# Retention in 64-token steps on 64x64 array tiles, with casting loads of q, k and weights on the Pool queue

## The chip, the core and the metric

The kernel runs on one core of a Trainium2 chip. The metric is the device time of one execution in microseconds (us): the median of three runs is 377.36 us (377.29 to 378.0).

## The reference

A retention layer (attention with an exponential decay in place of softmax) feeds a bilinear feed-forward block, written FFN below. q, k and v are float32 of shape [8, 8, 576, 64] (batch, head, sequence, head width); the weights are [512, 1536], [512, 1536] and [1536, 512].

```python
scores = scale * np.matmul(q, k.transpose(0, 1, 3, 2))
gamma = 1.0 - 2.0 ** (-5.0 - np.arange(H))
Dmat = np.where(rel >= 0, gamma[:, None, None] ** rel, 0.0)     # rel = i - j
attn = np.matmul(scores * Dmat, v)
x = attn.transpose(0, 2, 1, 3).reshape(B * S, H * D)            # [4608, 512]
out = ((x @ w_a) * (x @ w_b)) @ w_out
```

## The kernel before

The 4608 tokens are 36 chunks of 128. Two batches are nine chunks (PER = 9); the middle one (MID) holds the last 64 tokens of one batch and the first 64 of the next. The decay splits: v is scaled by gamma^-j (`vs`), the retention output by scale times gamma^i (`qs`), so that the products between need only a causal mask.

Retention of a chunk, heads in four pairs (HP):

- `load` (L97): q, k and v as float32 on SP's queue, three DMAs of 256 KB, each of 1024 runs of 256 B; five buffers of each.
- `cast` (L182): q and k to bf16 (for the first chunks on ACT and DVE, L187 and L188; later on POOL, L190 and L191), v times `vs` on POOL (L192).
- `transposes` (L199): eight 128x128 transposes on PE, then copies to `qkT`.
- `state` (L216): per head pair one product k^T v of 128 rows by 128 columns, summed over the chunks of a batch in one PSUM tile, whose two diagonal blocks ACT copies out (L232, L233).
- `scores` (L235): eight products, a head in each 64-row half of the array, masked by DVE (L250).
- `outputs` (L258): eight products of v with the masked scores (L267) and eight of the state with q (L276), each of 64 columns of the array; DVE multiplies by `qs` into `xT` (L282).

The FFN (`ffn_block`, L290) takes blocks of 512, 256, 384, 384 and then 512 tokens. Per block and each of 12 columns of 128 there are four matmuls into pa (L300) and four into pb (L313), ACT copies pa (L306), DVE multiplies (L318); then 12 matmuls per 128 tokens with w_out (L326), a copy to `osb` (ACT or DVE, L335 and L337) and a store on SP's queue (L338). One FFN matmul of 512 tokens is called a unit below: a block of 512 tokens has 144 of them, the kernel 1296.

What sets the order: the schedule is manual, so instructions stand on each engine as the code emits them. Chunks 0 to 3 come first, one after the other. The weights are loaded by casting DMAs on POOL's queue (`load_w`, `load_wo`). A small DMA (`gate`, L366) on SP's queue reads loaded w_out, so that SP's loads of chunks 4 and up wait for it. Later stages are placed among the FFN matmuls by `todo`, a list of places counted in units: chunks 4 to 8 one at a time (`one_by_one`), the others in pairs (`first_stage`: transposes and state; `second_stage`: state and scores; `third_stage`: outputs).

Of the kernel before, what the change touches and what calls it, by code (L numbers as in the profile page):

```python
# [18 lines left out]
def kernel(  # L19
# [18 lines left out]

    nc = tc.nc

    B, H, S, D = q.shape
    DM = H * D
# [9 lines left out]
    PER = 2 * S // 128  # L52
    MID = PER // 2
    HALF = S - 128 * MID
    assert HALF == 64 and NTOK % (2 * S) == 0

    def rows_of(i):

        b, m = 2 * (i // PER), i % PER
        if m < MID:  # L60
            return [(0, 128, b, 128 * m)]
        if m == MID:
            return [(0, 64, b, 128 * m), (64, 64, b + 1, 0)]
        return [(0, 128, b + 1, 64 + 128 * (m - MID - 1))]

# [6 lines left out]
    stage = pool("stage", 5)  # L72
    nat = pool("nat", 5)
    qkt_pool = pool("qkt", 4)
    st_pool = pool("st", 4)
    h_pool = pool("hT", 2)
    ha_pool = pool("ha", 6)
    o_pool = pool("osb", 4)
    PS = bass.MemoryType.PSUM
    ps_ffn = pool("ps_ffn", 3, PS)  # L80
    ps_att = pool("ps_att", 4, PS)
    ps_kv = pool("ps_kv", 1, PS)
# [3 lines left out]
    wa_r = moe_w_a.rearrange("(c p) f -> p c f", p=128)  # L86
    wb_r = moe_w_b.rearrange("(c p) f -> p c f", p=128)
    wo_r = moe_w_out.rearrange("(c p) m -> p c m", p=128)
# [3 lines left out]
    xT = big.tile([128, HP, NTOK], BF16)  # L92


    staged = {}

    def load(i):  # L97
        if i >= NCH:
            return
        tiles = []  # L100
        for name, src in (("qf", q), ("kf", k), ("vf", v)):
            t = stage.tile([128, DM], FP32, tag=name, name=name)
            for r0, n, b, s0 in rows_of(i):
                nc.sync.dma_start(  # L104
                    t[r0:r0 + n, :].rearrange("p (h d) -> p h d", h=H),
                    src[b, :, s0:s0 + n, :].rearrange("h s d -> s h d"))
            tiles.append(t)
        staged[i] = tiles

    for i in range(4):  # L110
        load(i)


    idxp_i = const.tile([128, PER], INT32)
    nc.gpsimd.iota(idxp_i[:, 0:MID + 1], pattern=[[128, MID + 1]], base=0,
# [3 lines left out]
    idx_i = const.tile([128, S + 64], INT32)  # L119
    nc.gpsimd.iota(idx_i[:, 0:S], pattern=[[1, S]], base=0,  # L120
                   channel_multiplier=0)
    nc.gpsimd.iota(idx_i[:, S:S + 64], pattern=[[1, 64]], base=0,
                   channel_multiplier=0)
    identity = const.tile([128, 128], BF16)
    make_identity(nc, identity)
    mask = const.tile([128, 128], BF16)
    nc.gpsimd.memset(mask, 1.0)
    nc.gpsimd.affine_select(
        out=mask, in_=mask, compare_op=ALU.is_ge, fill=0.0,
        base=0, pattern=[[1, 128]], channel_multiplier=-1)  # L130
    mask2 = const.tile([128, 128], BF16)
    nc.gpsimd.tensor_copy(mask2, mask)
    nc.gpsimd.memset(mask2[0:64, 64:128], 0.0)

    lgp = const.tile([128, HP], FP32)
    for c in range(HP):
        nc.vector.memset(lgp[0:64, c:c + 1], math.log(gammas[2 * c]))
        nc.vector.memset(lgp[64:128, c:c + 1], math.log(gammas[2 * c + 1]))
    biasq = const.tile([128, 1], FP32)
    nc.vector.memset(biasq, math.log(scale))  # L140
    idxp_f = const.tile([128, PER], FP32)
# [7 lines left out]
    idx_f = const.tile([128, S + 64], FP32)  # L149
    nc.vector.tensor_copy(idx_f, idx_i)  # L150
    qs = const.tile([128, HP, S + 64], FP32)

    def make_qs(c):
        nc.scalar.activation(qs[:, c, :], idx_f, AF.Exp,
                             bias=biasq[:, 0:1], scale=lgp[:, c:c + 1])

    states = [const.tile([128, HP, 128], BF16, name=f"state{i}")
              for i in range(4)]
    for t in states:
        nc.vector.memset(t, 0.0)  # L160
# [55 lines left out]
    def state(i):  # L216
        m = i % PER
        if m == PER - 1:
            return
# [259 lines left out]
```

## Time and profile before

| what | value |
|---|---|
| median of 3 runs | 377.36 us (377.29 to 378.0) |
| profiled execution: span from first to last instruction | 375.4 us; the median run is 2.0 us longer |
| PE busy | 345.6 us (92%) |
| DVE, ACT, POOL busy | 172.5, 127.9, 77.8 us |
| DMA: HBM read, written | 37.75 MB, 9.44 MB |
| retention products on PE | 1248 (288 transposes among them) |

The page has the busy share of each engine, its course over 40 slices of the span, the DMA queues, the chain of work that ended last, and groups of instructions by line. L300 is line 300 of the kernel; PE is the matmul engine, PEld its weight loads, SPq and POOLq are DMA issues. A matmul's printed duration covers its way through the pipeline; what it costs on a busy PE is the distance between two starts. A few matmul records are missing.

### The profile page before, as it was taken

The page shows a single profiled execution, that of the slowest core. Times are in us where ns is not written, and L with a number is a line of the kernel's source. Part 1 is how long each engine was busy: PE and PEld are TensorE (multiplying, and loading weights), DVE is VectorE, ACT ScalarE, POOL GpSimd, SP SyncE. Part 2 cuts the span into 40 slices and gives each one's busy share as a digit, 9 for nine tenths or more (in the row PEclk, how much of TensorE's full clock was granted, in tenths as well). Part 3 has the DMA queues.
Part 4 walks back from the last instruction along what each step waited for, and adds up shares of the span by engine and source line. Part 5 has one row for each costly group of instructions (what it writes and reads, how often), then busy time and mean ns, then how long its engine had stood idle before and what let it go on. Part 6 is the DMA issues. An engine that isn't in the chain of part 4 may idle for free.

```text
span 375.4 us, 6629 instructions
## 1 busy us (share of the span) xinstructions
PE 345.6 (92%) x2604; PEld 186.4 (50%) x2640; DVE 172.5 (46%) x292; ACT 127.9 (34%) x248; POOL 77.8 (21%) x113
## 2 busy tenths in 40 slices
PE   2669987777999999999999999999999999999995
PEld 1444443555565565455455545454545454544442
DVE  4542344454555546246434553455445544532421
ACT  7323313432452443244215422442244234303320
POOL 3550032542142230314031403040403000000000
PEclk9999999899999999999999999999999999999999
DMA  9999899957970890395039403950510020011002
GB/s 174 188 206 207 166 204 257 225 116 142 230 164 0 190 228 5 106 223 95 28 119 222 83 30 109 193 120 30 144 27 3 36 77 0 2 56 58 1 28 84
DMA packets 122511, 42.90 MB, mean 114 GB/s; under 512 B 113264, under 2 KB 117872, under 8 KB 122480
## 3 DMA queue, kind: packets, MB, share of 16 engines
q1 hardware_dynamic: 117728, 37.76, 47.5%
q0 software_dynamic: 4752, 4.72, 7.8%
q8 instruction: 20, 0.33, 0.4%
q14 instruction: 11, 0.09, 0.1%
HBM read 37.75 MB, written 9.44 MB: 126 GB/s over the span
## 4 chain that ended last, share of the span: by engine, by line
PE 78%; DMA 7%; SPq 6%; DVE 3%; issue 2%; POOL 1%; ACT 1%; DVEq 0%
PE po L326 23%; PE pa L300 22%; PE pb L313 21%; SPq L104 6%; DMA wo_sb<-in_moe_w_out_dram 5%; PE tp L204 4%; PE o L267 3%; DMA vf<-in_v_dram 3%; PE kv L227 2%; PE o L276 2%; DVE sT L250 1%; DVE hT L318 1%; ACT qkT L208 1%; DVE qkT L209 0%; POOL wa_sb L163 0%
## 5 line engine op out<-in xcount | busy, mean ns | idle before, releaser
L318 DVE TENSOR_TENSOR hT<-ha,pb 128x512 bf16<-128x512 bf16 (+2 forms) x120 | 76.1, 634 | 112.9 <-PE pb L313 106.8
L300 PE MATMUL pa<-xT,wa_sb 128*128 128x512 bf16 (+2 forms) x467 | 112.4, 364 | 2.9 <-DVE xT L282 1.6
L313 PE MATMUL pb<-xT,wb_sb 128*128 128x512 bf16 (+2 forms) x475 | 111.3, 359 | 0.2
L306 ACT CAST ha<-pa 128x512 bf16<-128x512 f32 (+2 forms) x120 | 65.1, 543 | 126.1 <-PE pa L300 112.6
L326 PE MATMUL po<-wo_sb,hT 128*128 128x512 bf16 x414 | 94.5, 379 | 2.0 <-issue 1.6
L192 POOL TENSOR_TENSOR vb<-vf,vs 128x512 bf16<-128x512 f32 x36 | 37.5, 1043 | 177.9 <-PE o L267 61.1
L313 PEld LDWEIGHTS <-wb_sb 128*128 128x128 bf16 x480 | 47.2, 98 | 46.8 <-issue 0.2
L300 PEld LDWEIGHTS <-wa_sb 128*128 128x128 bf16 x480 | 45.4, 99 | 45.8 <-issue 4.5
L326 PEld LDWEIGHTS <-hT 128*128 128x128 bf16 x432 | 40.8, 98 | 47.4
L337 DVE COPY osb<-po 128x512 f32<-128x512 f32 x17 | 11.8, 692 | 53.2 <-PE po L326 53.2
L335 ACT COPY osb<-po 128x512 f32<-128x512 f32 x19 | 11.1, 585 | 69.2 <-PE po L326 68.1
L282 DVE TENSOR_TENSOR xT<-o,qs 128x512 bf16<-128x512 f32 x36 | 24.3, 685 | 9.3 <-PE o L276 8.1
L267 PE MATMUL o<-sT,vb 128*64 128x128 bf16 x288 | 16.7, 231 | 7.6 <-DVE sT L250 7.4
L190 POOL CAST qb<-qf 128x512 bf16<-128x512 f32 x27 | 16.7, 618 | 23.1 <-issue 18.4
L204 PE MATMUL tp<-identity,qb 128*128 128x128 bf16 x144 | 15.0, 231 | 6.2 <-ACT qb L187 6.2
L267 PEld LDWEIGHTS <-vb 128*64 128x64 bf16 x288 | 11.0, 114 | 16.5 <-issue 13.1
L191 POOL CAST kb<-kf 128x512 bf16<-128x512 f32 x27 | 16.6, 613 | 8.7 <-DVE hT L318 4.0
L211 ACT COPY qkT<-tp 128x1024 bf16<-128x1024 bf16 x14 | 14.2, 1012 | 11.4 <-PE tp L204 11.4
L204 PE MATMUL tp<-identity,kb 128*128 128x128 bf16 x144 | 15.1, 232 | 1.5 <-DVE kb L188 1.5
L204 PEld LDWEIGHTS <-qb 128*128 128x128 bf16 x144 | 10.5, 102 | 11.1 <-ACT qb L187 7.4
L244 PEld LDWEIGHTS <-qkT 64*128 64x128 bf16 x288 | 8.8, 98 | 10.5 <-DVE qkT L209 8.2
L227 PE MATMUL kv<-vb,kb 128*128 128x128 bf16 (+1 forms) x128 | 13.3, 230 | 0.0
(197 smaller groups left out, 191.1 us busy)
## 6 DMA issues: line engine op xcount, KB each, us to landing
out_dram<-osb SPq DMA_DIRECT2D x36, 256.0 KB, 2.0
qf<-in_q_dram SPq DMA_DIRECT2D x32, 256.0 KB, 4.9
kf<-in_k_dram SPq DMA_DIRECT2D x32, 256.0 KB, 5.1
vf<-in_v_dram SPq DMA_DIRECT2D x32, 256.0 KB, 5.1
wo_sb<-in_moe_w_out_dram POOLq DMA_DIRECT2D x3, 512.0 KB, 17.4
qf<-in_q_dram SPq DMA_DIRECT2D x8, 128.0 KB, 4.1
kf<-in_k_dram SPq DMA_DIRECT2D x8, 128.0 KB, 3.6
vf<-in_v_dram SPq DMA_DIRECT2D x8, 128.0 KB, 4.1
```

The source lines that it names most:

```text
L104: nc.sync.dma_start(t[r0:r0 + n, :].rearrange("p (h d) -> p h d", h=H), src[b, :, s0:s0 + n, :].rearrange("h s d -> s h d"))
L190: nc.gpsimd.tensor_copy(qb, qf)
L192: nc.gpsimd.tensor_tensor(vb.rearrange("p (h d) -> p h d", h=H), vf.rearrange("p (h d) -> p h d", h=H), vs[:, i % PER, :].unsqueeze(2).to_ ...
L204: nc.tensor.transpose(tp[:, w, p, :], src[:, p * 128:(p + 1) * 128], identity)
L227: nc.tensor.matmul(kv[:, p, :], kb[r, sl], vb[r, sl], start=(m in (0, MID) and p == 0), stop=True, skip_group_check=True)
L267: nc.tensor.matmul(o[64 * hi:64 * hi + 64, p, :], vb[:, e0:e0 + 64], sT[:, hi, p, :], start=(p == 0), stop=(m == 0), skip_group_check=True)
L282: later.append(lambda: nc.vector.tensor_tensor(xT[:, :, i * 128:(i + 1) * 128], o, qs[:, :, s0:s0 + 128], op=ALU.mult))
L300: nc.tensor.matmul(pa[:, 0:n], wa_sb[:, c, fs], xT[:, c, tok0:tok0 + n], start=(c == 0), stop=(c == NC - 1))
L306: nc.scalar.copy(ha[:, 0:n], pa[:, 0:n])
L313: nc.tensor.matmul(pb[:, 0:n], wb_sb[:, c, fs], xT[:, c, tok0:tok0 + n], start=(c == 0), stop=(c == NC - 1))
L318: nc.vector.tensor_tensor(hT[:, F, 0:n], has[F][:, 0:n], pb[:, 0:n], op=ALU.mult)
L326: nc.tensor.matmul(po, hT[:, F, u * 128:(u + 1) * 128], wo_sb[:, F, :], start=(F == 0), stop=(F == NF - 1))
```

## The change

Retention is rewritten; the FFN's matmuls stay as they are.

- The step is 64 tokens. A chunk of 128 still is loaded at once and holds two steps, s = 0 and 1. Each product is 64 by 64 by 64 and uses one quarter of the array; four in a row use the four quarters. Per chunk there are 16 products k^T v, 16 scores (only within a step), 16 of v with scores, and 16 of the state with q: 2240 in the kernel. The state is no longer summed in PSUM: DVE adds each step's k^T v to a float32 sum (L268, L270), and ACT or POOL casts it to bf16 (`sbf`, L275, L277).
- q and k are loaded by casting DMAs on POOL's queue (L102) into a bf16 tile; the casts on ACT, DVE and POOL go. v stays on SP's queue.
- From chunk 6 on the transposes are DMAs on SP's queue (L231). The first six chunks keep the transposes on PE (L238).
- The chunk order is new: chunks 0 to 3 first, 4 and 5 singly in the first FFN block, then pairs (units[6] is chunks 6 and 7). `todo` has two places for a pair: `first` (stage1: state with q, scores; then the DMA transposes of the next pair, the scaling of v and the loads for later pairs) and `second` (stage2: the rest of the outputs; then k^T v of the next pair).
- The weight loads are cut into columns 0-255, 256-639, 640-1023, 1024-1535, each of four DMAs of 64 partitions; small DMAs (`hold`) on SP's queue make its loads of v wait for those of q. Heads stand in another order in `xT`, and the rows of w_a and w_b follow it.
- The FFN blocks are all 512 tokens, with block 1 cut in pieces (128, 128, 256, 256). PSUM: four tiles for the FFN instead of three. Eleven matmuls on zeros (`idle_products`) are added among the first chunks. The last store is split over two queues.

The diff, cut to its core:

```diff
+    def load_qk(i):
+        t = nat.tile([128, 2, DM], BF16, tag="qk", name="qk")
+        for w, src in ((0, q), (1, k)):
+            for r0, n, b, s0 in rows_of(i):
+                nc.gpsimd.dma_start(
+                    t[r0:r0 + n, w, :].rearrange("p (h d) -> p h d", h=H),
+                    src[b, :, s0:s0 + n, :].rearrange("h s d -> s h d"))
...
+    def transposes(i, by_dma):
...
+        if by_dma:
+            nc.sync.dma_start_transpose(
+                qkT.rearrange("p w c t -> p (w c) t"),
+                qk.rearrange("p w e -> p (w e)"))
+            return
...
+    def kv(unit, conv):
...
+                    for r in (0, 1):
+                        e = slice(64 * (2 * p + r), 64 * (2 * p + r) + 64)
+                        nc.tensor.matmul(ps[s][half(r), ci, p, :],
+                                         kb[half(s), e], vb[half(s), e],
+                                         start=True, stop=True,
+                                         skip_group_check=True)
...
+                nc.vector.tensor_tensor(new, ps[s][:, ci], last_sum[0],
+                                        op=ALU.add)
...
+    def from_state(o, ci, i, h, s, start):
+        r, p, c, j = h % 2, h // 2, h // 4, h % 4
+        u = 2 * i + s
+        st = state_of[u] if u % STEPS else zero_state
+        nc.tensor.matmul(o[s][half(c), ci, j, :], st[half(r), p, :],
+                         qkt_of[i][half(r), 0, p, half(s)],
+                         start=start, stop=True, skip_group_check=True)
...
+    def stage1(unit):
...
+                        nc.tensor.matmul(sc[r][half(s), ci, p, :],
+                                         qkT[half(r), 1, p, half(s)],
+                                         qkT[half(r), 0, p, half(s)],
...
+    def stage2(unit):
...
+                        nc.tensor.matmul(
+                            o[s][half(c), ci, j, :],
+                            vb[half(s), 64 * h:64 * h + 64],
+                            sT[half(s), h % 2, ci, h // 2, :],
...
+    idle_products(7)
+    for i in range(4):
+        vscale(i, nc.vector)
+        transposes(i, False)
+        kv((i,), nc.scalar)
+        flush()
+        if i == 0:
+            make_qs(0, EARLY)
+            load_w(0, 256)
+            load_w(256, 640)
+        if i:
+            stage2((i - 1,))
+        stage1((i,))
+        if i == 3:
+            idle_products(4)
+    stage2((3,))
+    hold(3, wa_sb[0:1, 0, 640 - 64:640])
...
+    def ahead(g):
+        if g + 1 < len(units) and g + 1 >= 6:
+            for i in units[g + 1]:
+                transposes(i, True)
...
+    def first(g):
+        flush()
+        stage1(units[g])
+        ahead(g)
+
+    def second(g):
+        flush()
+        stage2(units[g])
+        if 6 <= g + 1 < len(units):
+            kv(units[g + 1], nc.gpsimd)
...
+    todo = [(52, begin_single, (4,)), (58, first, (4,)), (68, second, (4,)),
+            (56, make_qs, (EARLY, QCOLS)),
+            (80, begin_single, (5,)), (86, first, (5,)), (94, second, (5,)),
+            (130, first, (6,)), (150, second, (6,))]
+    for g in range(7, len(units)):
+        p = 288 + 144 * ((units[g][0] - 8) // 4)
+        if units[g][0] % 4 == 0:
+            todo += [(p - 86, first, (g,)), (p - 66, second, (g,))]
...
+            todo += [(p - 40, first, (g,)), (p - 20, second, (g,))]
```

Two places show how the change moves instructions. The first is POOL's queue around the weight loads. Before, it holds the scaling of v (vb) and all weights, and no load of q or k (128x4x384 is the shape of a DMA; x3 means three alike in a row):

```order
L132 COPY mask_135<-mask 128x128
L133 MEMSET mask_135 64x64
L192 TENSOR_TENSOR vb<-vf,vs 128x512 x3
L163 DMA wa_sb<-in_moe_w_a_dram 128x4x384
L164 DMA wb_sb<-in_moe_w_b_dram 128x4x384
L192 TENSOR_TENSOR vb<-vf,vs 128x512
L163 DMA wa_sb<-in_moe_w_a_dram 128x4x512
L164 DMA wb_sb<-in_moe_w_b_dram 128x4x512
L163 DMA wa_sb<-in_moe_w_a_dram 128x4x640
L164 DMA wb_sb<-in_moe_w_b_dram 128x4x640
L167 DMA wo_sb<-in_moe_w_out_dram 128x4x512 x3
```

Now it holds the loads of q and k of chunks 0 to 3, then the weights up to column 1023, and then the following, of which the first two rows are chunk 4 (in two halves), the fifth and sixth chunk 5, the last two chunk 6:

```order
L102 DMA qk<-in_q_dram 64x8x64 x2
L102 DMA qk<-in_k_dram 64x8x64 x2
L118 DMA wa_sb<-in_moe_w_a_dram 64x4x512 x2
L118 DMA wb_sb<-in_moe_w_b_dram 64x4x512 x2
L102 DMA qk<-in_q_dram 128x8x64
L102 DMA qk<-in_k_dram 128x8x64
L124 DMA wo_sb<-in_moe_w_out_dram 128x4x512 x3
L439 IOTA idx_i 128x64
L441 IOTA idx_i 128x576
L443 IOTA idx_i 128x128
L102 DMA qk<-in_q_dram 128x8x64
L102 DMA qk<-in_k_dram 128x8x64
```

So chunks 4 and 5 have moved ahead of the last weights, and chunks 6 and 7 stand behind all of them in the same queue.

The second place is SP's queue behind the gate. Before, chunk 4 (in halves), then chunk 5, with q, k and v in turn:

```order
L104 DMA vf<-in_v_dram 128x8x64
L366 DMA gate<-wo_sb 1x16x4
L104 DMA qf<-in_q_dram 64x8x64 x2
L104 DMA kf<-in_k_dram 64x8x64 x2
L104 DMA vf<-in_v_dram 64x8x64 x2
L104 DMA qf<-in_q_dram 128x8x64
L104 DMA kf<-in_k_dram 128x8x64
```

Now v alone, and between the loads of v the transposes of chunks 6 and 7, then of 8 and 9, and so on:

```order
L138 DMA gate<-wa_sb 1x16x4
L110 DMA vf<-in_v_dram 64x8x64 x2
L110 DMA vf<-in_v_dram 128x8x64 x7
L231 DMA_TRANSPOSE qkT<-qk 128x8x128 x2
L110 DMA vf<-in_v_dram 128x8x64
L110 DMA vf<-in_v_dram 64x8x64 x2
L231 DMA_TRANSPOSE qkT<-qk 128x8x128 x2
L110 DMA vf<-in_v_dram 128x8x64 x2
L409 DMA out_dram<-osb 128x512 x4
```

The gate waits for columns up to 639 of w_a instead of for w_out; seven loads of v stand ahead of the first transposes, and the stores of a block's output queue behind transposes and loads of v.

544 lines of the change are left out of this document (264 added, 280 removed).

## The prediction

> **What bounds the kernel now.** I read the page first, for the busy shares and their course.
>
> ```profile
> span 375.4 us, 6629 instructions
> PE 345.6 (92%) x2604; PEld 186.4 (50%) x2640; DVE 172.5 (46%) x292; ACT 127.9 (34%) x248; POOL 77.8 (21%) x113
> PE   2669987777999999999999999999999999999995
> DMA  9999899957970890395039403950510020011002
> q0 software_dynamic: 4752, 4.72, 7.8%
> PE 78%; DMA 7%; SPq 6%; DVE 3%; issue 2%; POOL 1%; ACT 1%; DVEq 0%
> ```
>
> From the eleventh slice on (94 us) PE is full; before that DMA is, and PE has holes. So there are two stages with two limits. The table by windows (us; PE busy; ... ; granted clock, DMA share, GB/s) puts numbers to them, and the chain in order of time gives starts on PE.
>
> ```profile
> 4.00:16.00 12.00, 7.20 (x71) 5.09 (x72) 6.24 (x11) 6.76 (x12) 4.20 (x5) 1.00 1.34 218
> 20.00:40.00 20.00, 17.23 (x98) 8.57 (x96) 6.67 (x11) 5.53 (x11) 3.59 (x5) 1.00 1.23 206
> 26.42:95.00 68.58, 58.81 (x441) 32.76 (x446) 27.62 (x52) 21.78 (x45) 17.54 (x22) 0.98 0.96 189
> ```
>
> ```profile
> 12.34 4.93 DMA vf<-in_v_dram
> 22.06 17.37 DMA wo_sb<-in_moe_w_out_dram
> 156.28 0.86 PE pa L300 x4
> 158.88 0.86 PE pb L313 x4
> 181.73 6.85 PE po L326 x31
> 293.35 6.85 PE po L326 x31
> ```
>
> *The full stage.* From 156.28 to 158.88 twelve matmuls start: 0.217 us each; with the rounding of the starts I take 0.216 for a unit. The same place of the block comes three blocks later at 293.35: (293.35 - 181.73) / 3 = 37.21 us a block. Its 144 units are 31.10; the other 6.11 us are two pairs of chunks, 3.06 us a pair. All 1296 units are 279.9 us, which the change leaves.
>
> *The start.* The first FFN matmul comes at 26.42 us, and until 95 us PE is idle for 68.58 - 58.81 = 9.8 us. This is the timeline of PE, whose first two rows are the same product in two chunks:
>
> ```profile
> 17.54 0.29 PE L244 MATMUL sc_298<-qkT 64*128 64x128 bf16 x1 [1.14 <-DVE qkT L209]
> 22.64 0.29 PE L244 MATMUL sc_355<-qkT 64*128 64x128 bf16 x1 [1.14 <-DVE qkT L209]
> 26.42 0.58 PE L300 MATMUL pa<-xT,wa_sb 128*128 128x512 bf16 x1 [0.78 <-DVE xT L282]
> 27.23 4.12 PE L300 MATMUL pa<-xT,wa_sb 128*128 128x512 bf16 x10 [0.22 <-issue]
> 75.04 0.24 PE L267 MATMUL o<-sT,vb 128*64 128x128 bf16 x1 [0.46 <-DVE sT L250]
> 75.97 0.25 PE L267 MATMUL o<-sT,vb 128*64 128x128 bf16 x2 [0.69 <-DVE sT L250]
> ```
>
> A chunk takes 5.10 us, while the twelve loads of the first four chunks have landed at 12.34 + 4.93 = 17.27. Ten matmuls then take 4.12 us, about half speed. The two last rows are the waits of a chunk that is done alone among FFN matmuls: 1.15 us.
>
> **The full stage after the change.** These are PE rows of one pair:
>
> ```profile
> 196.45 0.39 PE L204 MATMUL tp<-identity,qb 128*128 128x128 bf16 x4
> 197.56 1.03 PE L300 MATMUL pa<-xT,wa_sb 128*128 128x512 bf16 x3
> 211.10 0.39 PE L267 MATMUL o<-sT,vb 128*64 128x128 bf16 x8
> 211.32 0.29 PE L276 MATMUL o<-qkT,state_165 128*64 128x64 bf16 x8
> 218.17 0.23 PE L244 MATMUL sc_2835<-qkT 64*128 64x128 bf16 x1
> 218.17 0.23 PE L244 MATMUL sc_2836<-qkT 64*128 64x128 bf16 x1
> 218.23 0.22 PE L244 MATMUL sc_2835<-qkT 64*128 64x128 bf16 x1
> ```
>
> and from the rows of line 276, one product 64 wide (min/median/max ns):
>
> ```profile
> L276 PE MATMUL o<-qkT,state_165 x8: 192/196/196, 211.3 to 211.4; 128*64 128x64 bf16 x8
> ```
>
> Before: 16 transposes and 4 whole products take 197.56 - 196.45 = 1.11 us, 0.0555 each. Products on half the array go two at a time: in two row halves both start at 218.17 and the next at 218.23; in two column halves eight start in 211.32 - 211.10 = 0.22 us, 0.028 each. A pair is 20 x 0.0555 + 4 x 0.0555 + 16 x 0.028 + 32 x 0.028 = 2.68 us. The rest of the 3.06, 0.38 us, I put to the passages between whole-array and part-array products, two visits a pair; the new kernel has two visits as well (`first`, `second`).
>
> After: 128 products, 32 groups of four. The eight 64-wide products of 211.32 print 0.29 us in all and 0.196 for one: seven distances in 0.094 us, 0.0135 each, 0.027 a couple. Four quarters at once are not in this trace. If they run together, a group costs as a couple does; the floor I set at 0.031, for 0.02 of rounding in 0.29. If only couples run together, 0.062. Both kinds of couple overlap in these rows, so I take 0.036, near the floor. A pair is 32 x 0.036 + 0.38 = 1.53 us (1.37 to 2.36), and fifteen pairs 23.0 us (20.6 to 35.5).
>
> The transposes' cover: they are issued in `first` of the pair before. For eight pairs (units 6, and every second one from 10) about 46 units lie between, 46 x 0.216 = 9.9 us and the products between, 11 us; for the others 98 units. A DMA transpose is not in this trace. Nearest is a load of 256 KB, on SP's queue:
>
> ```profile
> DMA to landing us min/median/max: 3.3/5.1/5.2
> ```
>
> It lands 3.3 us after issue alone and at most 5.2 behind others; in a row one comes every 1.2 us (256 KB at the 218 GB/s of the 4 to 16 us window). Two transposes at that price take 5 to 6.4 us, at four times the pieces 4 x 2.4 + 4 = 13.6. I take twice, 4.8 + 4 = 8.8 us, under 11; the upper end costs 2.6 x 8 = 21 us. The Trainium skill (DMA: Bandwidth & Descriptors, "Latency and other measured facts") gives 261 GB/s for DMA transposes; that would be an estimated 1.0 us for 256 KB and leave the sum as it is, and no run here shows it.
>
> DVE gains two adds a chunk and two halved multiplies each for masks and output. Rows by form:
>
> ```profile
> L318 DVE TENSOR_TENSOR hT<-ha,pb 128x512 bf16<-128x512 bf16 x84 | 57.8, 688 | 88.1 <-PE pb L313 86.7 <-PE pa L300 1.3
> L282 DVE TENSOR_TENSOR xT<-o,qs 128x512 bf16<-128x512 f32 x36 | 24.3, 685 | 9.3 <-PE o L276 8.1 <-PE o L267 1.2
> L318 DVE TENSOR_TENSOR hT<-ha,pb 128x256 bf16<-128x256 bf16 x12 | 5.0, 417 | 9.1 <-PE pb L313 6.7 <-ACT ha L306 2.4
> L209 DVE COPY qkT<-tp 128x512 bf16<-128x512 bf16 x9 | 3.8, 425 | 11.9 <-ACT qkT L208 11.9
> L154 ACT ACTIVATE qs<-idx_f,biasq,lgp 128x640 f32<-128x640 f32 x4 | 3.6, 912 | 0.0
> L163 POOL DMA_DIRECT2D wa_sb<-in_moe_w_a_dram x3 | 2.5, 838 | 0.0
> L337 DVE COPY osb<-po x2: 691/692/692, 366.4 to 371.6; 128x512 f32<-128x512 f32 x2
> ```
>
> In a block: 14 x 0.69 (hT, osb) + 8 x 0.685 (sT, xT) + 8 x 0.417 (adds) = 18.5 us of about 34: hidden, and DVE does the adds ahead of PE. POOL loses its casts and gets 80 loads of q and k at 0.84 us: eight a block, 6.7 us, hidden too. I allow 2 us (0 to 6) of waits.
>
> **The start after the change.** A casting load of 256 B runs is not in this trace. SP's loads, in the same runs, take 1.2 us; POOL's weights, counted in bf16, move 4.72 MB at 206 GB/s, 22.9 us. The lower end for a load of q or k is 1.2 us, as uncast; the upper 2.0, if each run of 256 B costs two thirds more; I take 1.4, nearer the row with the same runs.
>
> *FFN start.* Loads begin at about 1 us (before: 17.27 - 11 x 1.2 - 3.3 = 0.8) and the first lands 3.3 us later, at 4.3. Seven more casts and four loads of v: 4.3 + 7 x 1.4 + 4 x 1.2 = 18.9 us (17.5 to 23.1) for the fourth chunk. DVE per chunk: 0.685 + 0.425 + 6 x 0.417 = 3.6 us, less than the 4.0 of its loads; the loads set the pace where the engines' 5.10 did. Behind the last landing: eight transposes at half speed 0.9, copy 0.4, two adds 0.8, a cast 0.4, two masks 0.8, two multiplies 0.8, 16 groups at half speed 1.2, the four matmuls on zeros past the masks 4 x 0.41 - 0.8 = 0.8, handovers 0.5: 6.6. FFN start 25.5 (24 to 30), at full clock.
>
> *The next wait.* `second` of chunk 5 puts k^T v of chunks 6 and 7 into PE's queue ahead of FFN block 1. PE is there after 96 units (20.7), chunks 4 and 5 on PE (2 x 1.6: eight transposes, 16 groups, passages) and waits like those of 75 us (2 x 1.15), and 1.0 for ACT, which makes the rest of `qs` in about 4 x 1.05 us while four PSUM tiles cover 3.5: 25.5 + 20.7 + 3.2 + 2.3 + 1.0 = 52.7. The data need all that stands ahead on the DMA engines: 16 casts, nine loads of v (four buffers beyond v4 are free at once) and the weights: 4.3 + 15 x 1.4 + 9 x 1.2 + 22.9 = 59.0 us (56.0 to 68.0). As a test, before's twelve loads and two thirds of w_out come by this to 17.27 + 20.3 = 37.6; the trace has 22.06 + 17.37 = 39.43. So PE waits 6.3 us there and goes on at 59.0. What hid the loads of chunks 6 and 7, the FFN's first block, no longer covers them.
>
> *The sum.* 59.0 + 1200 x 0.216 (259.2) + 23.0 + waits 2 + tail. The tail goes from the last copy's start, 371.6, to 375.4, 3.8 us, less 0.69 - 0.42 for the halved copy: 3.5. Span 346.7; with the 2.0 us that the median (377.36) has beyond this span, 348.7 us. Ends: 56.0 + 259.2 + 20.6 + 0 + 3.5 + 2.0 = 341.3; 68.0 + 259.2 + 35.5 + 6 + 3.5 + 2 = 374.2. If the data never bind, 52.7 takes the place of 59.0 at floor prices: 338.
>
> **The rivals.**
>
> *Dear ends (13%).* Couples only (62 ns a group) add 15 x 0.83 = 12.5 us: 361. Casting loads at 2.0 us: 358. Both: near 370. For: neither is in the trace. Against: each kind of couple overlaps, and the queues are the same 16 engines'.
>
> *Late transposes: slower (9%, 2 of it between 360 and 376).* Their two DMAs take over 11 us, and PE, in order, stands before the scores of eight pairs. The gain of 28.7 us is gone at 3.6 us a pair, 7.3 us a transpose; at 8 us each, 5 x 8 = 40: 389 us. For: SP's queue is shared with v and the stores, and the DMA share, 0.96 until 95 us, leaves no room there. Against: the slices' DMA row is at 0 to 5 for most of the later span.
>
> *Starts that don't come closer (4%).* If a product can't start sooner than 28 ns after the one ahead (the mean at 211.10), whatever its width, a pair is 128 x 0.028 + 0.38 = 3.96 us: 348.7 + 15 x 2.43 = 385. Against: 64-wide ones start 13.5 ns apart. The Trainium skill (TensorE: Matmul & The Clock Gate, "Wait — 56ns, not 53.3ns?") says that start-to-start never drops below about 25 ns however small the product. The rows at 211.32 contradict that for products in different tiles, so it keeps this chance alone.
>
> *No gain (3%).* The quarters overlap and the start only swaps one wait for another, late by 20 us or more: 376 to 378.
>
> **How the numbers follow.** The forecast's own range, 338 to 361, has 71%; the time is its likeliest, 349. With the dear ends and half-late transposes, up to 372, it is 86%; what lies above is left out. A measurement can tell 0.2%, 0.75 us. Faster: 71 + 13 + 2 = 86%; same 3%; slower 7 + 4 = 11%.
>
> **What would show it.** Right: groups of four starts within 31 to 40 ns in `stage1`; blocks of 34.2 us; FFN start at 24 to 27 us; a hole on PE ahead of L257 near 53 to 59 us whose releaser is the load of q or k. Wrong: products 13 ns apart or more (couples), holes at L310 or L290 released by the DMA transposes, POOL's DMA rows far over 0.84 us, or a DMA row full to the end.

## The result, and the profile after

The changed kernel takes 357.41 us, the median of four runs (356.52 to 358.02), beside 377.68 for the kernel before, measured together with it: a ratio of 0.9465 (95% interval 0.9441 to 0.9488), so 5.3% faster. The forecast was 349 us, with 338 to 361 as its own range and 372 as the end with dear ends and half-late transposes in it. The execution that was profiled is one of 358.02 us with a span of 356.3. Executions of one and the same kernel differ by 1.4 to 3.4 us below, and as only one of each was traced, the cause is not shown; changes of that size are called unclear.

From the page of the changed kernel, the rows that answer to those of before:

```profile
span 356.3 us, 8899 instructions
...
PE 329.1 (92%) x3739; PEld 168.3 (47%) x3739; DVE 167.6 (47%) x321; ACT 93.5 (26%) x179; POOL 133.4 (37%) x196
...
PE   5559877599999999999999999999999999999995
...
DMA  9999999999999990996199929966930140011002
...
q0 software_dynamic: 80944, 14.16, 51.2%
...
PE 84%; DMA 4%; DVE 4%; POOL 3%; issue 3%; ACT 1%; POOLq 0%; SPq 0%; DVEq 0%
```

There are two stages as before, the first now eight slices long (71 us). POOL's queue, q0, now takes 51.2% of the DMA engines' time, where it took 7.8%, and in the chain POOL and DVE stand where SP's queue stood. The window from the first FFN matmul to 95 us (PE busy first; granted clock, DMA share and GB/s at the end):

```profile
28.28:95.00 66.72, 57.17 (x656) 34.53 (x656) 28.22 (x63) 20.81 (x45) 38.28 (x50) 0.95 1.52 164
```

PE is idle there for 66.72 - 57.17 = 9.55 us, beside 9.8 before; the first FFN matmul comes at 28.28, 1.9 us later than before, and the granted clock on record is 0.95 in place of 0.98. (The record begins at 33.6 us here and at 30.9 before; what lies ahead of that is printed as full clock, though the matmuls run at half speed there.) So the start has gained nothing. All of the gain is in the full stage. There the timeline of PE has the same visit one block apart:

```profile
163.45 0.32 PE L290 MATMUL o<-qkT,sbf 64*64 64x64 bf16 x16
163.60 0.43 PE L310 MATMUL sc<-qkT 64*64 64x64 bf16 x32
...
174.20 0.26 PE L290 MATMUL o<-qkT,sbf 64*64 64x64 bf16 x8 [0.27 <-POOL sbf L277]
...
198.18 0.32 PE L290 MATMUL o<-qkT,sbf 64*64 64x64 bf16 x16
```

One of the 32 scores takes 0.193 us by its own row (min/median/max ns):

```profile
L310 PE MATMUL sc<-qkT x32: 192/193/194, 163.6 to 163.8; 64*64 64x64 bf16 x32
```

A block is 198.18 - 163.45 = 34.73 us, against 37.21. Less 31.10 for its 144 units and 0.46 for the one wait in it (from 173.74 to 174.20, for POOL's cast of a sum), two pairs are left with 3.17 us: 1.59 a pair. Before it was 3.06, and fifteen pairs make (3.06 - 1.59) x 15 = 22.1 us, a little more than the whole gain. The 32 scores run in 0.43 us, of which the last one takes 0.193: 0.237 / 31 = 7.6 ns from one start to the next on the mean, 31 ns for four. That is the floor of the prediction. The single starts in the trace come in fours, mostly 3 to 4 ns apart, with 20 to 22 ns between one four and the next.

The start, in the timeline of PE; each row's bracket is the wait ahead of it:

```profile
28.28 1.86 PE L365 MATMUL pa<-xT,wa_sb 128*128 128x512 bf16 x4 [0.85 <-DVE xT L349]
...
44.59 0.31 PE L257 MATMUL kv<-vb,qk 64*64 64x64 bf16 x8 [1.00 <-DVE vb L219]
...
51.32 0.62 PE L332 MATMUL o<-sT,vb 64*64 64x64 bf16 x16 [2.44 <-DVE sT L318]
...
55.28 0.32 PE L257 MATMUL kv<-vb,qk 64*64 64x64 bf16 x16 [1.00 <-DVE vb L219]
...
60.36 0.32 PE L257 MATMUL kv<-vb,qk 64*64 64x64 bf16 x16 [0.47 <-POOL vb L219]
...
61.35 0.32 PE L257 MATMUL kv<-vb,qk 64*64 64x64 bf16 x16 [0.68 <-POOL vb L219]
...
68.90 0.59 PE L365 MATMUL pa<-xT,wa_sb 128*128 128x128 bf16 x4 [3.85 <-DVE hT L378]
```

At 60.36 and 61.35 stands k^T v of chunks 6 and 7. The data had come: k of chunk 7, issued on POOL at 43.13, took the longest of these landings, 14.3 us, and was there at 57.45.

```profile
L102 POOL DMA_DIRECT2D qk<-in_k_dram x2: 873/874/876, 43.1 to 47.3; - x2
...
DMA to landing us min/median/max: 11.9/13.6/14.3
```

What PE waited for was POOL's product of v and its decay, `vscale`. The longest wait, 3.85 us before 68.90, looks like one for DVE's product `hT`. The timeline of DVE shows that DVE itself stood, in order, in front of an add that waited for a buffer:

```profile
68.23 0.42 DVE L270 TENSOR_TENSOR s<-kv,s 128x256 f32<-128x256 f32 x1 [3.96 <-POOL sbf L277]
```

And the timeline of POOL shows why the cast (L277) that frees the buffer came so late:

```profile
57.49 0.87 POOL L102 DMA_DIRECT2D qk<-in_q_dram  x1 [0.63 <-PE pb L373]
...
59.25 4.04 POOL L219 TENSOR_TENSOR vb<-vf,vs 128x512 bf16<-128x512 f32 x4
63.23 0.94 POOL L102 DMA_DIRECT2D qk<-in_q_dram  x1
64.17 0.89 POOL L102 DMA_DIRECT2D qk<-in_k_dram  x1
65.04 1.39 POOL L102 DMA_DIRECT2D qk<-in_q_dram  x2
66.39 1.40 POOL L102 DMA_DIRECT2D qk<-in_k_dram  x2
67.73 1.48 POOL L277 CAST sbf<-s 128x256 bf16<-128x256 f32 x4
```

Four products of v and six issues of loads stood ahead of four casts of 0.37 us. None of them was slow; they were in the way.

### The profile page after: what moved, and what is told of

Its sections match the earlier page's. It is cut to its first block, busy times and chain, and to the rows that moved or that the text cites. A ratio compares the mean times of both kernels' runs of the same rounds, so it can differ in the third digit from the quotient of the medians.

```text
span 356.3 us, 8899 instructions
## 1 busy us (share of the span) xinstructions
PE 329.1 (92%) x3739; PEld 168.3 (47%) x3739; DVE 167.6 (47%) x321; ACT 93.5 (26%) x179; POOL 133.4 (37%) x196
## 3 DMA queue, kind: packets, MB, share of 16 engines
q0 software_dynamic: 80944, 14.16, 51.2%
## 4 chain that ended last, share of the span: by engine, by line
PE 84%; DMA 4%; DVE 4%; POOL 3%; issue 3%; ACT 1%; POOLq 0%; SPq 0%; DVEq 0%
PE pa L365 26%; PE pb L373 26%; PE po L390 25%; DMA vf<-in_v_dram 3%; POOL qk L102 2%; PE o L332 2%; PE o L290 2%; PE kv L257 2%; DVE s L270 1%; DMA qk<-in_q_dram 1%; PE sc L310 1%; DVE hT L378 1%; ACT qs L193 1%; DVE vb L219 1%; POOL vb L219 1%
## 5 line engine op out<-in xcount | busy, mean ns | idle before, releaser
L277 POOL CAST sbf<-s 128x256 bf16<-128x256 f32 x53 | 21.0, 403 | 154.7 <-DVE s L270 103.8
L102 POOL DMA_DIRECT2D qk<-in_q_dram x40 | 35.0, 877 | 8.5 <-issue 4.0
L102 POOL DMA_DIRECT2D qk<-in_k_dram x40 | 34.2, 859 | 8.0 <-DMA qk<-in_q_dram 4.9
L349 DVE TENSOR_TENSOR xT<-o,qs 128x512 bf16<-128x512 f32 (+1 forms) x42 | 23.8, 608 | 8.7 <-PE o L290 4.5
L318 DVE TENSOR_TENSOR sT<-sc,keep 128x512 bf16<-128x512 f32 (+1 forms) x42 | 23.8, 609 | 7.7 <-PE sc L310 7.6
L270 DVE TENSOR_TENSOR s<-kv,s 128x256 f32<-128x256 f32 x56 | 23.6, 421 | 7.0 <-POOL sbf L277 4.0
L290 PE MATMUL o<-qkT,sbf 64*64 64x64 bf16 x512 | 16.2, 201 | 7.3 <-DVE xT L349 5.0
L290 PEld LDWEIGHTS <-sbf 64*64 64x64 bf16 x512 | 10.9, 111 | 14.2 <-ACT sbf L275 5.6
L257 PE MATMUL kv<-vb,qk 64*64 64x64 bf16 x512 | 9.9, 203 | 6.5 <-DVE vb L219 5.4
L332 PE MATMUL o<-sT,vb 64*64 64x64 bf16 x576 | 10.1, 200 | 2.5 <-DVE sT L318 2.4
```

Of the source, the lines that this page charges most:

```text
L102: nc.gpsimd.dma_start(t[r0:r0 + n, w, :].rearrange("p (h d) -> p h d", h=H), src[b, :, s0:s0 + n, :].rearrange("h s d -> s h d"))
L270: nc.vector.tensor_tensor(new, ps[s][:, ci], last_sum[0], op=ALU.add)
L290: nc.tensor.matmul(o[s][half(c), ci, j, :], st[half(r), p, :], qkt_of[i][half(r), 0, p, half(s)], start=start, stop=True, skip_group_check ...
L318: nc.vector.tensor_tensor(sT[:, r].rearrange("p n c t -> p (n c) t"), sc[r].rearrange("p n c t -> p (n c) t"), keep.unsqueeze(1).to_broadc ...
L332: nc.tensor.matmul(o[s][half(c), ci, j, :], vb[half(s), 64 * h:64 * h + 64], sT[half(s), h % 2, ci, h // 2, :], start=False, stop=True, sk ...
L349: nc.vector.tensor_tensor(view(xT, t0), o[s].rearrange("p n j t -> p j n t"), view(qs, c0), op=ALU.mult)
```

## The experiments

**Transposes back on PE.** The pairs' transposes leave SP's queue and are PE's again.

```diff
 for i in units[g + 1]:
-    transposes(i, True)
+    transposes(i, False)
```

> One part undone: the transposes of chunks 6 to 35 are on PE again, with copies on ACT and DVE. Theory (the DMA transposes are hidden, and every transpose on PE is on the path): 15 pairs x 16 x 0.0555 = 13.3 us more, about 370.7 us, and no hole at the scores. Rival (the DMA transposes cost the kernel waits of their own, or the copies take the place of the products): no more than 5 us above 357.4.

Measured: 370.71 us, ratio 0.9832 (0.9811 to 0.9854). In PE's timeline the sixteen of a pair:

```profile
168.95 1.07 PE L238 MATMUL tp<-identity,qk 128*128 128x128 bf16 x16
```

0.9 us to the next start, 15 times 13.3 us: the loss is the work itself, and the DMA transposes in its place cost the full stage nothing that shows. They are two thirds of the gain.

**Four products in a row on one quarter.** Only the order of the loops over products changes, in `kv`, the scores and v x sT, from one that goes round the quarters to one that stays on a quarter for four (two for the products from the state); here that of the scores:

```diff
-for p in range(HP):
-    for r in (0, 1):
-        for s in (0, 1):
+for r in (0, 1):
+    for s in (0, 1):
+        for p in range(HP):
             nc.tensor.matmul(sc[r]...
```

> The same products in another order: those that follow each other use the same quarter of the array (by fours in the scores, k^T v and v with scores, by twos from the state). Theory (four quarters run together, one quarter takes 0.028 us a product): of 16 products 13 stand in a row, 0.36 us for 0.124, so a pair costs 8 x 0.24 = 1.9 us more, 28 us over 15 pairs, about 385 us. Rival (starts are spaced 8 ns apart by issue and not by the quarters): under 2 us more.

Measured: 361.09 us, ratio 0.9577 (0.9551 to 0.9604), about 4 us and not 28.

```profile
163.18 0.52 PE L310 MATMUL sc<-qkT 64*64 64x64 bf16 x32
```

(0.52 - 0.193) / 31 = 10.5 ns a start in place of 7.6. So the quarters overlap in this order too, and my theory of a strict order was wrong.

**Eight in a row.** The same, with both chunks of a pair inside, so that eight products (four from the state) follow on one quarter.

> The order of the products again, now with eight in a row in one quarter (scores, k^T v, v with scores) or four (from the state), over both chunks of a pair. Fours cost 3.7 us where 28 were expected; in the trace of that run two products of one quarter start 7 ns apart. Theory (a quarter takes 0.027 us a product, but PE begins products a few places ahead, so that short runs are evened out): runs of eight are no longer evened out, 128 products come near 0.020 to 0.027 us each, 1.5 to 2.5 us a pair more, 22 to 37 us in all. Rival (a product of 64 columns in one quarter is just cheap, about 0.011 us): as with fours, under 6 us more than 357.4.

Measured: 373.18 us, ratio 0.9889 (0.9855 to 0.9922): 16 us more than the changed kernel.

```profile
166.23 0.84 PE L311 MATMUL sc<-qkT 64*64 64x64 bf16 x31
```

(0.84 - 0.193) / 30 = 21.6 ns a start. The starts and visits of this trace make a pair 2.71 us, and 15 x (2.71 - 1.59) = 17 us is what the time shows. Three orders of the same 32 products give 7.6, 10.5 and 21.6 ns: four quarters do work at once, and a quarter is a resource that can be queued for. The single starts of the 32 scores say at what price: the first five are 31 to 32 ns apart, and then they come mostly in couples, 5 to 6 ns and 25 to 27 ns apart. So a quarter takes a product every 31 to 32 ns, and the couples fit a next run of eight that begins beside the one ahead, some three products early. That PE looks a few products ahead for one whose quarter is free would explain why runs of four cost so little; it isn't shown by itself.

**Six buffers for the sums.** The wait before 68.90 hangs on three buffers of float32 sums, which POOL's late casts hold.

```diff
-s32_pool = pool("s32", 3)
+s32_pool = pool("s32", 6)
```

> Six buffers for the float32 sums of the state in place of three. Theory (near 64 us DVE can't add because the sum three back still waits for its cast, which stands on POOL behind the scaling of v and the loads, and PE waits for DVE): 4 us less, about 353.4 us, and the hole of 4.07 us on PE goes. Rival (the cast is late whatever the buffers, and PE meets it at the next products from the state): within 1 us of 357.4.

Measured: 356.68 us, ratio 0.9465 (0.9446 to 0.9485): no change that can be told, as the rival had it. The 3.85 us are gone from the trace, so the buffers were their cause; but PE runs on into the next late thing, the DMA transposes of chunks 6 and 7, and ahead of that it waits 1.27 us, where it was 0.47, for POOL's `vscale`.

```profile
73.66 0.26 PE L290 MATMUL o<-qkT,sbf 64*64 64x64 bf16 x8 [1.51 <-DMA qkT<-qk]
```

**v without its gates.** The gates hold the loads of v on SP until q of the chunk before has landed; v of chunk 3 landed 6 us after k of the same chunk.

```diff
-hold(0, qk_of[0][0:1, 0, 0:64])
 load_v(1)
```

(and so for chunks 2 and 3)

> The three small DMAs that make SP's loads of v of chunks 1 to 3 wait for those of q are left out; v is loaded at once. Theory (the FFN starts at 28.3 and not at 25.5 because v of the fourth chunk lands at 21.7 behind weights): FFN start about 26 us, and 2 us less at the end, about 355.4 us. Rival (the loads only change places, and the end is set further on): FFN start earlier, the end within 1 us of 357.4.

Measured: 355.70 us, ratio 0.9435 (0.9409 to 0.9461): 1.1 us by the ratios, unclear. v of chunk 3 now lands at 10.11 us, but FFN doesn't begin earlier: it begins at 29.44 us (in the two runs with six sums and with `qs` in parts, which change no load ahead of FFN, at 29.02 and 29.62). What v gains on the DMA engines, q and k lose: k of chunk 0 lands at 9.08 us in place of 6.32. The long wait for DVE's `hT` is 1.79 and not 3.85 us there, and no half clock follows it; but the 2.34 us ahead of v x sT of chunk 4 are followed by half clock, from 53.0 to 59.8 us.

**The late `qs` in four parts.** Each Exp of 1.0 us goes to a unit of its own (40, 48, 56, 64), not all four to unit 56.

```diff
-(56, make_qs, (EARLY, QCOLS)),
+(40, make_qs, (EARLY, QCOLS, (0,))), (48, make_qs, (EARLY, QCOLS, (1,))),
+(56, make_qs, (EARLY, QCOLS, (2,))), (64, make_qs, (EARLY, QCOLS, (3,))),
```

> The later part of qs is made in four places of the first FFN block, eight units apart, in place of one. Theory (PE's hole of 2.8 us at 48.5 comes from the four Exp in a row on ACT, behind which a copy of pa waits, behind that DVE's product and its masks): the hole shrinks to under 1.3 us, FFN block 1 begins about 1.5 us sooner, and the end follows by 0 to 1.5 us, since the v products of chunk 6 on POOL (59.2 us) set the next start. Rival (the hole is the latency of the scores and masks): hole unchanged.

Measured: 356.71 us, ratio 0.9461 (0.9438 to 0.9484): unclear. The 2.44 us before v x sT of chunk 4 are gone, but PE stands longer at the next place, and 3.86 us for `hT` as before:

```profile
61.32 0.32 PE L258 MATMUL kv<-vb,qk 64*64 64x64 bf16 x16 [1.38 <-POOL vb L220]
```

**Zeros in the waits ahead of FFN.** Twelve idle products where PE waits in chunk 3, to keep the clock up.

```diff
 transposes(i, False)
+if i == 3: idle_products(5)
 kv((i,), nc.scalar)
```

(and 4 and 3 more behind `kv` and `stage2` of chunk 3)

> Twelve more matmuls on zeros, where PE waits for chunk 3: five behind its transposes, four behind its k^T v, three behind its last products. Theory (the twelve FFN matmuls at 0.427 us from 28.3 to 33.4 are slow since PE stood still too much before): they go at 0.216 and 2.5 us are gained there; at the end 0 to 2 us less, since POOL's v products at 59.2 us set the next start. Rival (the zeros push the FFN start back by as much as the clock gains): FFN start 1 to 2.5 us later, end unchanged.

Measured: 356.81 us, ratio 0.9459 (0.9436 to 0.9481): unclear. FFN begins at full clock, 1.02 us for four matmuls where the changed kernel took 1.86,

```profile
28.88 1.02 PE L365 MATMUL pa<-xT,wa_sb 128*128 128x512 bf16 x4
```

and 3.02 us of wait follow before 68.54 all the same. Instead there is half clock, 0.50 from 49.1 to 59.4 us, behind another wait, of 2.69 us, where the changed kernel has none:

```profile
49.55 0.71 PE L332 MATMUL o<-sT,vb 64*64 64x64 bf16 x16 [2.69 <-DVE sT L318]
```

Three repairs, six sums, `qs` in parts and zeros, each of which removes the loss that it aims at, move the time by less than 1 us: behind each stands another wait for late POOL or late data, or another stretch at half clock.

**All of them at once,** with `vscale` of chunks 6 to 9 on DVE as well:

```diff
-vscale(i, nc.gpsimd)
+vscale(i, nc.vector if i < 10 else nc.gpsimd)
```

> Together: six sums, v not held, qs spread, zeros in the waits, and the scaling of v of chunks 6 to 9 on DVE and not on POOL. Theory (the 8.7 us by which the forecast was too low are all in the first 75 us, as waits that follow each other, and no edit alone frees the next one): PE is past the k^T v of chunks 6 and 7 at about 56 us and has no hole over 1.5 us behind it; 6 to 9 us less, about 350 us. Rival (the loads set that start, whatever the engines do): 2 to 3 us less, about 355 us.

Measured: 353.45 us, ratio 0.9377 (0.935 to 0.9405). That is 4 us less, between the theory's 6 to 9 and the rival's 2 to 3, and the mechanism is the rival's: with POOL out of the way the wait is the one that the prediction had named, at nearly its time: k of chunk 7.

```profile
59.77 0.43 PE L255 MATMUL kv<-vb,qk 64*64 64x64 bf16 x16 [2.87 <-DMA qk<-in_k_dram]
60.13 0.61 PE L363 MATMUL pa<-xT,wa_sb 128*128 128x128 bf16 x4
```

In the window behind it the clock is 0.50:

```profile
59.80:61.80 2.00, 2.00 (x32) 1.94 (x33) 0.53 (x2) 0.38 (x2) 1.89 (x3) 0.50 1.81 136
```

The groups of four that should take 0.217 us take 0.425, fourteen of them.

**Zeros in that wait.** Thirteen idle products between chunk 5 and k^T v of chunks 6 and 7.

```diff
 stage2(units[g])
+if g == 5:
+    idle_products(13)
```

> The kernel with all the ramp changes at once (353.45 us), and thirteen idle products of 0.216 us each put on TensorE between the last products of chunk 5 and k^T v of chunks 6 and 7, where it waited 2.87 us for the data of chunk 7 and then ran fourteen groups of four products at 0.425 us in place of 0.217 (2.9 us lost). Theory, that the half clock follows from the wait before it: the groups run at 0.217 and the time falls to 350.5 (349.5 to 351.5). Rival, that the half clock comes from what TensorE runs there (loads of weights for products of 128 columns) and not from the wait: it stays, and the time is 353 to 354.5.

Measured: 355.75 us, ratio 0.9424 (0.9399 to 0.9449). The mechanism is right and the time is not.

```profile
58.09 2.98 PE L200 MATMUL idle_ps<-idle 128*128 128x512 bf16 x13
...
61.38 0.40 PE L363 MATMUL pa<-xT,wa_sb 128*128 128x128 bf16 x4
...
78.53 0.26 PE L255 MATMUL kv<-vb,qk 64*64 64x64 bf16 x2 [2.70 <-issue]
```

The groups run at full clock and the same place of the block comes 1.3 us earlier, although FFN began 1.4 us later in this execution: 2.7 us gained, as the theory has it. Then PE stands for 2.7 us in k^T v of chunks 8 and 9, for nothing that the profile shows, and the window behind that has half clock:

```profile
78.60:80.60 2.00, 2.00 (x7) 0.79 (x7) 0.00 (x0) 0.00 (x0) 0.00 (x0) 0.50 2.09 146
```

What this wait is stays open. One lead: a 16 KB packet of the instruction queue (q8) is under way from 75.29 to 76.92 us; that PE waits for its instructions there is not shown.

**Nothing ahead of its data.** All of the above but the thirteen zeros, and k^T v of chunks 6 and 7 no longer in front of FFN that could run:

```diff
-(80, begin_single, (5,)), (86, first, (5,)), (94, second, (5,)),
-(130, first, (6,)), (150, second, (6,))]
+(74, turn, (5,)), (82, sums, (5,)), (86, first, (5,)), (94, second, (5,)),
+(112, kv, (units[6], nc.scalar)), (160, first, (6,)), (180, second, (6,))]
```

(`turn` and `sums` are the two halves of `begin_single`; chunk 4 has them at 50 and 58; `second` of chunk 5 no longer calls `kv`)

> The same kernel (353.45 us) with nothing but the places of the retention steps in the first blocks changed: k^T v of chunks 6 and 7 no longer stands right behind chunk 5 (unit 94) but at unit 112, their scores at 160 and not 130, their second step at 180 and not 150, and the transposes of chunks 4 and 5 stand 8 units ahead of their k^T v, not right ahead of it. Theory, that PE's queue waits for late data while 24 units of FFN that need nothing stand behind the wait: the waits of 1.9 and 1.2 us at chunks 4 and 5 and the 2.87 us at chunk 7 go, and the 2.9 us of half clock with them, in sum 8.9 us: 344.6 (343 to 347). Rival, that the data, the sums' casts on POOL or the transposes of chunks 6 and 7 are the bound whatever stands where: the waits come back at another place, and the time is 350 to 354.

Measured: 350.16 us, ratio 0.9298 (0.9271 to 0.9324), the fastest of all, 5.6 us above the theory's 344.6 and in the rival's range. The wait for k of chunk 7 is gone and so is all half clock behind the first 25 us. What comes back, in a trace of the slowest of the six executions, 353.15 us:

```profile
54.05 0.26 PE L288 MATMUL o<-qkT,sbf 64*64 64x64 bf16 x8 [1.37 <-ACT sbf L273]
...
87.44 0.22 PE L288 MATMUL o<-qkT,sbf 64*64 64x64 bf16 x2 [2.54 <-DMA qkT<-qk]
```

The second wait is for the two transposes of chunks 8 and 9, issued from 74.03 on:

```profile
DMA to landing us min/median/max: 7.9/9.8/11.7
```

They are part of `first` of chunks 6 and 7, which I had moved from unit 130 to 160, and so their cover went from 72 units to 42. That was my own slip: a step that is moved takes its DMAs with it.

**Float32 loads and casts.** Back to the changed kernel, with the second half of the change undone: q and k as float32 on SP, three chunks ahead and without the gates among the first four, cast by ACT and DVE, from chunk 6 on by POOL.

```diff
-nc.gpsimd.dma_start(t[r0:r0 + n, w, :]...
+nc.sync.dma_start(f[r0:r0 + n, w, :]...
...
+nc.scalar.copy(t[:, 0], f[:, 0])
+nc.vector.tensor_copy(t[:, 1], f[:, 1])
```

> The changed kernel with its casting loads undone: q and k come as float32 on SP's queue, three chunks ahead, without the gates between the first four chunks, and are cast by ScalarE and VectorE for the first six chunks and by POOL for the others. To be read beside the kernel without those gates (355.70 us), which casts in the loads. Theory, that both loads are paced by the memory and the casts hide: 354 to 358.5, no difference that can be told. First rival, that the loads were what the casting saved: the float32 loads at 1.2 us each and the casts on ScalarE and VectorE delay chunks 4 to 7, and each late microsecond is one of the time: 360 to 365. Second rival: the casting loads cost more than they save (POOL's issue, 0.88 us each, ahead of the sums' casts), and the time falls under 353.

Measured: 376.36 us, ratio 0.9979 (0.9963 to 0.9995): the whole gain is gone, far past every number that I had written down.

```profile
34.84 0.61 PE L252 MATMUL tp<-identity,qk 128*128 128x128 bf16 x4 [9.20 <-ACT qk L114]
```

This is PE's wait for the cast of q of chunk 2; one of 4.66 us for that of k follows. On POOL's timeline the weights begin, and on SP's queue the load of k of chunk 2 has this row, and both of its loads this time to landing:

```profile
2.60 1.43 POOL L136 DMA_DIRECT2D wa_sb<-in_moe_w_a_dram  x2
```

```profile
L103 SPq DMA_DIRECT2D qf<-in_k_dram x1: 4109/4109/4109, 17.2 to 17.2; - x1
...
DMA to landing us min/median/max: 22.3/22.3/22.4
```

With no loads of q and k ahead of them, POOL's weights are issued from 2.60 us on (10.22 in the changed kernel), and the loads of the first chunks, on another queue, take up to 22.4 us to land (k of chunk 2 is there at 39.59). FFN begins at 51.95. So this run changed the order of the data as well as their form.

**The same in order.** On POOL the weights wait for k of chunk 2, and SP's loads of chunks 4, 5 and 6 follow gates on weights.

```diff
+nc.gpsimd.dma_start(gate[:, 1, :], qf_of[2][0:1, 1, 0:64])
 load_w(0, 256)
```

> As the kernel with float32 loads of q and k on SP (376.36 us), but with the data in the order of the changed kernel: on POOL the first weights wait for k of chunk 2, and on SP the loads of chunks 4 and 5 follow a gate on the weights' first 640 columns as before, chunk 6 one on their last columns. Theory, that the float32 loads themselves cost little and the 19 us were the weights overtaking chunks 1 to 3 (k of chunk 3 landed at 43.6 us, FFN began at 50.9): k of chunk 3 lands at 16 to 18 us, FFN begins at 26 to 30, and the time is 354 to 361. Rival, that q and k as float32 on SP are slow whatever the order (1.2 us each, the casts ahead of the transposes, SP's queue waiting for buffers): FFN begins after 33 us, or chunks 4 to 7 come late by more than 5 us, and the time is 364 to 372.

Measured: 365.69 us, ratio 0.9682 (0.9656 to 0.9709). Of the 19 us that the float32 loads had cost, 10.7 were the order. FFN begins at 30.75, 2.5 us later than in the changed kernel; then chunk 4 is late:

```profile
49.74 0.61 PE L253 MATMUL tp<-identity,qk 128*128 128x128 bf16 x4 [5.44 <-ACT qk L114]
...
DMA to landing us min/median/max: 11.5/15.6/19.6
```

Its four loads of q and k take 11.5 to 19.6 us from issue to landing. In the changed kernel the same four loads, in POOL's queue ahead of the last weights, take

```profile
DMA to landing us min/median/max: 8.9/9.2/9.5
```

and land at 29.73 to 33.49 us, here at 45.54 to 49.98. Again it is the order: on two queues the weights, issued freely by POOL, go on landing while SP's loads wait. The Trainium skill (DMA: Bandwidth & Descriptors, "SWDGE vs HWDGE vs iDMA") says that each DMA engine goes round the queues of both kinds in turn; the late landings agree with that as far as they go. The form has its part too. The longest wait of this run is the chain that cost the changed kernel 3.85 us, and here four casts of q and k, which casting loads do without, stand among what is ahead of the sums' casts on POOL:

```profile
78.20 0.59 PE L388 MATMUL pb<-xT,wb_sb 128*128 128x128 bf16 x4 [6.43 <-DVE hT L393]
```

What float32 loads cost if every byte came in the changed kernel's order has not been measured. What is left is 8 us beside the changed kernel and 10 beside the one without gates (355.70), and how it divides between order and form is not shown.

## Why the prediction was right, and what it missed

The sign, the size and the two stages were right; the time came out 8.4 us above the forecast, inside the range. Of the four signs that were to show it, two came, the groups of four starts in 31 ns and a block of 34.73 us for 34.2, and two did not: FFN began at 28.28 us and not at 24 to 27, and the wait ahead of L257 ended with POOL's `vscale` and not with a load. By its steps:

- *A pair in the full stage, 1.53 us: right.* Measured 1.59; fifteen pairs are 0.9 us over the term. That it is so near is in part luck: the scores' groups of four take 31 ns and not 36, but 32 groups at 31 ns leave 0.60 us for the passages, for which the prediction had 0.38. (Part of that is k^T v, whose 32 starts are some 11 ns apart.)
- *DMA transposes hidden: right, but at another price.* I took 8.8 us for two. Each takes SP 1.2 to 3.9 us and lands 3.1 to 10.2 us after its issue; two in a row take from 4.6 to 12.7 us, over 10 us in six pairs of fifteen:

```profile
L231 SPq DMA_TRANSPOSE qkT<-qk x30: 1231/1444/3893, 61.9 to 290.1; - x30
...
DMA to landing us min/median/max: 3.1/6.3/10.2
```

  The rival "late transposes" did not come to pass, though four pairs took the 11 us that it asked for: none made PE wait. The cover is thin: where it was 42 units, above, PE waited 2.54 us. (In the changed kernel it is 44 to 46 or 98 units, and 72 for chunks 8 and 9, which the prediction left out.) The Trainium skill's 261 GB/s (DMA: Bandwidth & Descriptors, "Latency and other measured facts"; for a middle dimension that is not contiguous) is an estimated 1.0 us for 256 KB. As a rate the trace does not speak against it, with two landings as little as 0.85 us apart; as the time of one transpose it is not seen, the quickest took 3.1 us to land.
- *Starts no closer than 28 ns: refuted* by 7.6 ns across quarters.
- *Casting loads at 1.4 us each: too dear.* From chunk 6 on they land 0.88 us apart (54.59 to 60.78 for eight), 7 to 17 us behind their issues. The rival's 2.0 was further off.
- *FFN start at 25.5 us, at full clock: too early, and the clock wrong.* It is 28.28, and its first twelve matmuls take 0.427 us each (2.5 us). The 6.6 us behind the last landing hold (28.28 - 21.71); but that landing is v of chunk 3, behind its gate, at 21.71 and not at 18.9. Nor do the loads alone set the pace: a chunk takes the engines 4.15 us (14.76 to 18.91 for the same product in chunks 1 and 2), the four Exp for `qs` on ACT, 3 us ahead of the copy of chunk 1's transposes, were not in the sum, and of the lateness of v only 1.2 us is a wait of DVE.
- *PE at k^T v of chunks 6 and 7 at 52.7, data at 59.0: both wrong, in opposite ways.* PE came there at 59.9: 2.8 from FFN's start, 2.5 from the clock, 1.3 from waits of 4.6 us in chunks 4 and 5 in place of 3.3, and 0.6 in their own work. The data were there at 57.45. FFN went on at 61.6, 2.6 us behind the forecast, because the engines were late and not the data; that it is so near is luck. Only once those were repaired was k of chunk 7 the wait.
- *POOL "hidden too", "DVE does the adds ahead of PE", "2 us (0 to 6) of waits": the step that failed.* I took POOL's load by its sum over a block and left out its order. In the start four products of v and six issues of 0.7 to 0.9 us each stand ahead of four casts; the casts hold three buffers, the buffers hold DVE, DVE holds PE: 3.85 us, and behind it 2.8 us at half clock.

Against the forecast span of 346.7 these are 2.2 us (61.6 with k^T v done, for 59.0 without it), 3.85, 2.8 and 0.9: 9.75, of the 9.6 that the span has more. In the full stage the waits allowed for, 2 us, were 1.9 (0.46 three times and 0.53).

Where the gain comes from is shown in part by taking parts away: of the 22.1 us of the full stage the transposes are 13.3. The other 8.8 are what is left for the products in smaller tiles; no run takes these away alone, but with eight in a row on a quarter, 16 us more, they would be a loss. The casting loads put q, k and weights into one queue, in the order in which they are needed, and spare POOL the casts of q and k; the first was worth 10.7 us between two runs with float32 loads, and what the second is worth is not measured by itself.

## What to carry to other kernels

An engine that issues DMAs and also computes has one queue: list what stands in it ahead of each short instruction, not only its busy time, and ask which buffers that short instruction holds. In a stage that several late things bind together, repairs one by one can show nothing; make them together, and look which wait is then left. Loads that move to another queue change the order in which everything lands, and that can weigh more than their own cost.

## What the runs showed of the hardware

- A 64x64 product for another quarter of the array starts mostly 3 to 4 ns after the one ahead, and one quarter takes a product every 31 to 32 ns: 7.6 ns a start on the mean going round the four, 21.6 ns with eight in a row on one.
- Half clock follows from how PE's work falls into steps of 3.41 us, and not from a wait's length alone. In all fourteen traces the stretches between two changes of the granted clock are whole multiples of 3.413 us. Cut along these steps, the wait of 3.85 us in the changed kernel (first row; half clock from 67.74 on) and that of 3.43 us in the run with eight in a row (the other two; no half clock) look like this:

```profile
64.33:67.74 3.41, 0.72 (x12) 0.60 (x11) 0.00 (x0) 0.53 (x2) 3.41 (x6) 1.00 1.40 118
...
63.95:67.37 3.42, 1.60 (x28) 1.45 (x26) 0.82 (x4) 0.99 (x4) 3.42 (x6) 1.00 2.08 120
67.37:70.78 3.41, 1.80 (x33) 1.80 (x33) 1.78 (x7) 0.84 (x4) 3.41 (x7) 1.00 1.71 130
```

  The first wait leaves PE 0.72 us of work in one step; the second is split over two. The others go the same way: half clock came behind the waits of 2.70, 2.87 and 3.02 us, whose steps had 0.71, 1.19 and 1.06 us of work, and not behind the 2.54 us of the fastest kernel, with 1.91 and 2.38. In all traces a step at full clock with up to 1.2 us of work was followed by half clock and one with 1.7 us or more was not; between the two both happened. Full clock came back only after a step with 2.6 us of work or more. The Trainium skill (TensorE: Matmul & The Clock Gate, "Part 1: The HAM clock gate") gives an idle window of about 3.4 us. The length agrees with the steps here; but a step did not have to be idle throughout.
- Zero products can hold the clock up: with twelve of them ahead of FFN the record shows full clock from 25.0 to 27.3 us on in four traces, and from 32.5 to 34.3 us on in eight without them; thirteen in the data wait kept it at 1.00. Such a wait then costs once and not twice.
- The issue of a load of q or k takes POOL 0.68 to 1.08 us in the changed kernel (median 0.90 for q), and POOL stands between issues as well while earlier loads are still landing; what is queued behind waits along. A row of the kernel with all repairs at once:

```profile
44.48 0.88 POOL L102 DMA_DIRECT2D qk<-in_q_dram  x1 [1.93 <-DMA qk<-in_k_dram]
```
